# Batch 1 of an FFT-filter and MLP kernel: last first-stage store in two halves, second-stage pieces 0.6 steps later

## The chip, the core and the metric

The kernel runs on one core of one Trainium2 chip. The metric is the device time of one execution in microseconds (us). Before the change the median of three runs is 776.99 us (776.98 to 777.12). The profiler's engines are TensorE (PE, with its weight loads PEld), VectorE (DVE), ScalarE (ACT), GpSimd (POOL) and SyncE (SP). SP only issues DMAs here, and POOL mostly does.

## The reference

Eight sequences of 3008 rows and 256 channels are filtered along the sequence in the frequency domain. The result goes, row by row, through an MLP with a "snake" activation:

```
X = rfft(x, axis=1)                    # x: 8 x 3008 x 256
y = irfft(X * (filt_r + 1j*filt_i))    # 8 x 3008 x 256 -> 24064 rows of 256
h = y @ w_in                           # 256 -> 2048
g = h + sin(alpha*h)**2 / alpha
out = g @ w_out                        # 2048 -> 256, float32
```

## The kernel before

**The filter as matmuls.** A length of 3008 is 47 x 64, so each batch's transform is done in two stages, and its inverse in two more. Batch 0 has a path of its own and stays on chip. Batch 1 goes through HBM twice, by these pieces of the class `Spectral`:

- `first(i)`, i = 0 to 15: one matmul over 47 rows (line 206, tile pa) for two of the 32 row groups, then an eviction by `evac` into the tile t1_h. Four of them make a chunk; the fourth (j == 3) issues the store of the chunk's 8 row groups to the HBM tile d1, on SP (line 211, 384 KB).
- `load_t2(g)`, g = 0 to 3: POOL loads a quarter of d1, turned, into t2 (line 235). As each quarter reads all of d1's row groups, it waits for all four stores.
- `forward(u)`, u = 0 to 11: two matmuls (line 243, tile pb), an ACT eviction into xf (line 246), and two SP copies that swap the halves of xf into xs (line 250).
- `product(u)` and `cross(u)`: three VectorE operations (lines 257, 263, 264) that multiply with the filter and leave p.
- `inverse(u)`: two matmuls of p (line 274, tile pc) and an ACT eviction into g. Every third one issues two SP stores of g to the HBM tile d2 (line 281).
- `load_t4(ch)`: SP loads d2 into t4 (line 306). `last(u)`, u = 0 to 15: the matmuls of the last inverse stage (line 316, tile pd), evicted into y, the MLP's input.

Batches 2 to 7 do the same with packed matmuls in `first_tiled` (line 222, stores at line 229) and `inverse_tiled`. Batch 0's last stage is `last_0` (line 403, tile pd, too). Its late pieces are spread between MLP matmuls one by one.

**The MLP as the beat.** The rows are cut into 48 chunks. `hidden(k, jb)` makes one 128-wide block of the hidden layer: two matmuls (line 601, tile ph), the sine on ACT (line 605, tile cos_all), and VectorE's combination of both into v (line 606). `project(k, u)` makes eight matmuls of the second layer (line 621, tile po). ACT copies finished blocks to o (line 630), and POOL issues their stores to the output (line 665). A *step* is two `hidden` of chunk k and one `project` of chunk k-1 (none in some steps behind a chunk of 384 rows instead of 512, and none in chunk 0). Eight steps make a chunk, so step 18 belongs to chunk 2 and step 38 to chunk 4. In the names of tiles ph_2_4 is block 4 of chunk 2, made in step 18.

**Who sets the order.** All instructions are issued in the order in which the code records them; each engine works through its own in order. Pieces of the batches are put on a list with a due time in steps, by `put`. `slot(at)` runs after a step's hidden pair (at = step) and after its projections (at = step + 0.5), and issues what is due, in order of due time. It stops when a second PE piece turns up that is due later than at - 1, and whatever stands behind that piece waits for the next slot as well. `clear` and `aside` move times a little where a piece of batches 2 to 7 stands close.

For batch 1 the times are: `first(i)` at 6.9 + 0.35 i, `load_t2` at 12.5, `inverse(u)` at inv = 24 + 1.21 u, `forward(u)` at inv - 6, `product(u)` half a step after it and `cross(u)` four steps after it, `load_t4` at 38.5 (three chunks) and 45, `last(u)` from 43 on. Batch 2's first `first_tiled` is due at 37.5.

**Shared buffers.** The pieces' PSUM tiles come in turn from the pool fps, with two buffers; the tiles ph from hps, with four. `first_tiled` takes two of each. A matmul into a buffer waits until the tile before in it has been read: by ACT or VectorE for fps, by VectorE's v for ph.

Of the kernel before, what the change touches and what calls it, by code (L numbers as in the profile page):

```python
# [23 lines left out]
NK = 4 * NS  # L24
# [47 lines left out]
def kernel(  # L72
# [10 lines left out]
    nc = tc.nc  # L83
# [41 lines left out]
    t1_h = [cpool.tile([128, 16, C], FP16, name=f"t1_h{i}") for i in range(2)]  # L125
# [13 lines left out]
    for h in range(2):  # L139
        nc.sync.dma_start(out=x32[:, 4 * C * h:4 * C * h + 4 * C],  # L140
                          in_=bass.AP(tensor=x.tensor, offset=x.offset + 4 * h * C, ap=[[32 * C, 96], [1, 4 * C]]))
# [40 lines left out]
    def evac(dst, src, on_act=None):  # L182
        flip[0] = (flip[0] + 1) % 3
        if flip[0] if on_act is None else on_act:
            marks["act"] = nc.scalar.copy(out=dst, in_=src)  # L185
        else:
            marks["dve"] = nc.vector.tensor_copy(out=dst, in_=src)  # L187

    class Spectral:
# [13 lines left out]
        def first(self, i):  # L203
            ch, j = divmod(i, 4)
            ps = fps.tile([128, 512], FP32, name=f"pa_{self.b}_{i}", tag="f")
            marks["pe"] = nc.tensor.matmul(out=ps[0:NK, :], lhsT=wf_t, rhs=self.x[ch][:, 2 * j:2 * j + 2, :],  # L206
                                           start=True, stop=True)
            r0 = 8 * (ch % 2)
            evac(t1_h[ch // 2][0:NK, r0 + 2 * j:r0 + 2 * j + 2, :], ps[0:NK, :])
            if j == 3:  # L210
                nc.sync.dma_start(out=self.d1_rows[:, 8 * ch:8 * ch + 8, :], 
                                  in_=t1_h[ch // 2][0:NK, r0:r0 + 8, :])

        def first_tiled(self, ch):
            r0 = 8 * (ch % 2)
# [141 lines left out]
    for g in range(2):  # L357
        gs = slice(12 * g, 12 * g + 12)
        for k, filt in enumerate((filt_r, filt_i)):
            for q in range(2):  # L360
                if (g, k, q) == (0, 1, 1):
# [3 lines left out]
                    out=f_t[k][64 * k + 32 * q:64 * k + 32 * q + 32, gs, :],  # L365
                    in_=bass.AP(tensor=filt.tensor, offset=filt.offset + off,
                                ap=[[N1 * C, 32], [step, 12], [1, C]]))
# [167 lines left out]
    for jb in range(0, 16, 8):  # L535
        ins = nc.sync.dma_start(out=w_out32[:, jb:jb + 8],
                                in_=moe_w_out[128 * jb:128 * jb + 1024].rearrange("(b p) c -> p b c", p=128))
# [133 lines left out]
    def put(at, fn, *args, pe=False):  # L671
        pending.append((at, len(pending), pe, fn, args))

    def firsts(b):

        return {2: (37.5, 39.5, 41.5, 43.5), 3: (49.5, 54.5, 60.5, 66.5)}.get(
            b, [48 * b - 105.5 + 8 * ch for ch in range(4)])

    def inverses(b):

        return (63.5, 73.5, 81.5) if b == 2 else [48 * b - 46.5 + 16 * w for w in range(3)]
# [3 lines left out]
    def clear(at):  # L685

        return next((s + 1 for s in bursts if s - 0.75 < at <= s + 0.25), at)

    def aside(at):

        return next((s + 0.05 for s in bursts if s - 1.1 < at <= s), at)
# [9 lines left out]
    for b in range(1, B):  # L701
        s = s1 if b == 1 else Spectral(b)
        z = 48 * b
        if b > 1:
            for ch in range(4):
                put(22 + 4 * ch if b == 2 else firsts(b)[ch] - 8, s.load_x, ch)
        if b < TILED:
            for i in range(16):
                put(6.9 + 0.35 * i, s.first, i, pe=True)
        else:  # L710
            for ch in range(4):
                put(firsts(b)[ch], s.first_tiled, ch, pe=True)
        for g in range(4):
            put(12.5 if b == 1 else 45 if b == 2 else max(70, z - 77 + 12 * g), s.load_t2, g)
        for u in range(12):
            inv = 24 + 1.21 * u if b == 1 else 57 + 2.2 * u if b == 2 else z - 59 + 4 * u
            fwd = inv - 6
            fwd = clear(fwd)
            put(fwd, s.forward, u, pe=True)
            put(aside(fwd + (0.5 if b == 1 else 1.5)), s.product, u)  # L720
            if s.fused:
                put(aside(fwd + (4 if b == 1 else 4.5)), s.cross, u)
            if b < TILED:
                put(inv, s.inverse, u, pe=True)
        if b >= TILED:
            for w in range(3):
                put(inverses(b)[w], s.inverse_tiled, w, pe=True)
        for ch in range(4):
            put(z - (9.5 if b == 1 and ch < 3 else (10.5, 10.5, 10.5, 3)[ch]), s.load_t4, ch)
        for u in range(16):  # L730
            put(clear(z + (u - (5 if b == 1 else 6.5) if u < 4 else 2 * u - 9 if b == 1 else 2.6 * u - 11)),
                s.last, u, pe=True)
# [59 lines left out]
```

## Time and profile before

| what | value |
|---|---|
| median of 3 runs | 776.99 us |
| profiled execution, its own time | 779.76 us |
| its span, first to last instruction | 778.0 us |
| granted TensorE clock, mean | 0.997 |
| HBM traffic over the span | 132 GB/s |
| MLP matmuls, lines 621 and 601, busy | 389.9 us and 389.1 us |
| v on VectorE, line 606, mean of one | 671 ns |
| sine on ACT, line 605, mean of one | 600 ns |
| t2 loads, line 235, median from issue to landing | 5.2 us |

In the lines below, a row of a timeline gives the start in us from the span's start, the duration of the group in us, the engine, the line, the operation with output <- input, the shapes, the count, and in brackets idle time of the engine before it with what ended that. "SPq" is a DMA issue on SP. A row of the waits gives the engine and piece that waited, what it waited for, the total in us, the count and the longest. A row of the windows gives, for a stretch, each engine's busy time in the order PE, PEld, DVE, ACT, POOL, and then the granted clock, the share of the DMA engines' time, and GB/s. Starts of matmuls that follow each other closely overlap by about 0.1 us in the records, so lengths of blocks are read from start to start.

### The profile page before, as it was taken

Reading aid. Unit: us, or ns where it says so; the run is one execution under the profiler, and the core shown is the slowest. Engines: PE = TensorE matmul, PEld = TensorE weight load, DVE = VectorE, ACT = ScalarE, POOL = GpSimd, SP = SyncE. Lnnn points to the kernel's source line nnn. Section 1 sums busy time; section 2 is a strip of 40 time slices with the busy share of each in tenths; the row PEclk is TensorE's granted clock in tenths of the full one; section 3 lists DMA queues with packets and bytes.
Section 4 is the critical chain, followed back from the end, with each engine's and each line's share of the span. In section 5 each row is a group of like instructions: output and inputs, shape, how many; then the busy total and the mean of one; then the engine's idle time right before and its main releaser. Section 6 shows DMA issues by size and latency. Waiting matters only on the chain.

```text
span 778.0 us, 17230 instructions
## 1 busy us (share of the span) xinstructions
PE 764.5 (98%) x6039; PEld 517.0 (66%) x6039; DVE 658.0 (85%) x1174; ACT 610.4 (78%) x1204; POOL 370.4 (48%) x649
## 2 busy tenths in 40 slices
PE   7999999999999999999999999999999999999997
PEld 3757766666666666666666666766666666766665
DVE  6986998999988888898889988898888888787773
ACT  5798888898878877888878787788778787777762
POOL 6355555634555655455464647554454645430000
PEclk9999999999999999999999999999999999999999
DMA  9955578864765428644474536864254322511112
GB/s 223 267 108 160 119 181 242 220 137 124 187 165 133 124 58 219 154 108 127 107 194 121 139 95 145 198 152 120 72 145 110 87 70 56 135 46 34 37 41 56
DMA packets 81518, 101.49 MB, mean 130 GB/s; under 512 B 18884, under 2 KB 60864, under 8 KB 81431
## 3 DMA queue, kind: packets, MB, share of 16 engines
q0 software_dynamic: 27440, 47.29, 26.1%
q1 hardware_dynamic: 53434, 52.79, 25.4%
q8 instruction: 47, 0.77, 0.4%
q10 hardware_dynamic: 557, 0.31, 0.2%
q14 instruction: 40, 0.33, 0.1%
HBM read 56.15 MB, written 46.66 MB: 132 GB/s over the span
## 4 chain that ended last, share of the span: by engine, by line
PE 91%; DVE 5%; ACT 1%; issue 1%; DMA 1%; ACTq 0%; DVEq 0%
PE po L621 40%; PE ph L601 40%; DVE v L606 3%; PE pd L316 2%; PE pb L243 2%; PE pa L222 2%; PE pc L293 1%; ACT cos_all L605 1%; PE pc L513 1%; DMA w<-in_moe_alpha_dram 1%; PE warm L437 1%; PE pb L491 1%; PE pa L459 1%; PE pa L206 0%; PE pd L403 0%
## 5 line engine op out<-in xcount | busy, mean ns | idle before, releaser
L606 DVE SCALAR_TENSOR_TENSOR v<-cos_all,ph 128x512 f16<-128x512 f32 (+1 forms) x768 | 482.5, 671 | 99.2 <-ACT cos_all L605 95.7
L605 ACT ACTIVATE cos_all<-ph 128x512 f32<-128x512 f32 (+1 forms) x768 | 413.9, 600 | 101.8 <-PE ph L601 98.5
L665 POOL DMA_DIRECT2D out_dram<-o x530 | 291.7, 557 | 244.1 <-ACT o L630 215.3
L621 PE MATMUL po<-w,v 128*128 128x256 f16 x3008 | 389.9, 273 | 0.9 <-DVE v L606 0.9
L601 PE MATMUL ph<-y,w 128*128 128x512 f16 (+1 forms) x1536 | 389.1, 375 | 1.3 <-DVE v L606 1.1
L621 PEld LDWEIGHTS <-v 128*128 128x128 f16 x3008 | 289.9, 98 | 85.9 <-DVE v L606 1.5
L601 PEld LDWEIGHTS <-w 128*128 128x128 f16 x1536 | 143.1, 98 | 114.0 <-issue 19.1
L630 ACT COPY o<-po 128x512 f32<-128x512 f32 (+1 forms) x95 | 56.1, 591 | 7.6 <-PE po L621 6.9
L246 ACT CAST xf<-pb 128x512 f16<-128x512 f32 x84 | 51.1, 608 | 2.0 <-PE pb L243 1.2
L185 ACT CAST y<-pd 128x376 f16<-128x376 f32 (+1 forms) x86 | 42.1, 491 | 12.3 <-PE pd L316 8.8
L160 POOL DMA_DIRECT2D x<-in_x_dram x48 | 25.6, 538 | 40.1 <-DVE v L606 26.8
L185 ACT CAST t_h<-pa 128x512 f16<-128x512 f32 (+1 forms) x60 | 32.8, 590 | 12.5 <-PE pa L222 11.3
L316 PEld LDWEIGHTS <-t_a 96*128 96x128 f16 x448 | 31.4, 97 | 12.7
L264 DVE TENSOR_TENSOR p<-p,xs 128x512 f16<-128x512 f16 x84 | 35.7, 425 | 2.9
L263 DVE TENSOR_TENSOR xs<-xs,filt_t 128x512 f16<-128x512 f16 x84 | 35.1, 418 | 1.6 <-DMA xs<-xf 1.6
L257 DVE TENSOR_TENSOR p<-xf,filt_t 128x512 f16<-128x512 f16 x84 | 35.0, 417 | 0.0
L185 ACT CAST gt<-pc 128x512 f16<-128x512 f32 x54 | 28.1, 595 | 8.4 <-PE pc L293 8.4
L187 DVE CAST t_h<-pa 128x512 f16<-128x512 f32 (+1 forms) x52 | 33.5, 682 | 0.2
L243 PE MATMUL pb<-t,d_t 128*128 128x256 f16 x168 | 32.1, 273 | 0.6 <-ACT cos_all L605 0.6
L316 PE MATMUL pd<-wh_t,t_a 96*128 96x94 f16 x384 | 31.8, 204 | 0.0
L235 POOL DMA_DIRECT2D t<-d x28 | 24.4, 874 | 12.0 <-DMA d<-t_h 10.9
L243 PEld LDWEIGHTS <-d_t 128*128 128x128 f16 x168 | 16.3, 98 | 15.1 <-DMA t<-d 0.8
(70 smaller groups left out, 278.0 us busy)
## 6 DMA issues: line engine op xcount, KB each, us to landing
t<-d POOLq DMA_DIRECT2D x28, 384.0 KB, 5.2
xs<-xf SPq DMA_DIRECT2D x168, 64.0 KB
t_a<-d SPq DMA_DIRECT2D x28, 384.0 KB
x<-in_x_dram POOLq DMA_DIRECT2D x50, 188.0 KB, 4.5
d<-t_h SPq DMA_DIRECT2D x48, 192.0 KB
d<-gt SPq DMA_DIRECT2D x36, 256.0 KB
out_dram<-o POOLq DMA_DIRECT2D x91, 64.0 KB, 2.1
out_dram<-o POOLq DMA_DIRECT2D x31, 80.0 KB, 3.6
```

What stands on the lines that cost most here:

```text
L185: marks["act"] = nc.scalar.copy(out=dst, in_=src)
L243: nc.tensor.matmul(out=ps[:, i, :], lhsT=d_t[:, s, :], rhs=self.t2[s // 6][:, s % 6, :], start=True, stop=True)
L246: nc.scalar.copy(out=self.xf[u], in_=ps)
L263: nc.vector.tensor_tensor(out=xs, in0=xs, in1=f_t[1][:, 2 * u:2 * u + 2, :], op=ALU.mult)
L264: nc.vector.tensor_tensor(out=p, in0=p, in1=xs, op=ALU.add)
L316: nc.tensor.matmul(out=psv[:, i, :], rhs=wi_t if self.b < TILED else wh_t, start=True, stop=True, lhsT=t4_h[ch // 2][0:NK, n0 % 16 + i, cb ...
L601: nc.tensor.matmul(out=ps[:, 0:n], lhsT=w1[:, cb, jb * 128:jb * 128 + 128], rhs=y_cols[:, cb, c0:c0 + n], start=(cb == 0), stop=(cb == 1))
L605: nc.scalar.activation(out=cs[:, 0:n], in_=ps[:, 0:n], func=AFT.Sin, bias=float(np.pi / 2))
L606: marks["snake"] = nc.vector.scalar_tensor_tensor(out=v[k][:, jb, 0:n], in0=cs[:, 0:n], scalar=-1.0, in1=ps[:, 0:n], op0=ALU.add, op1=ALU. ...
L621: nc.tensor.matmul(out=pso[k][:, t % 2, :], lhsT=v[k][:, jb, 128 * t:128 * t + 128], rhs=w2[:, jb, :], start=(jb == 0), stop=(jb == 15))
L630: copy(out=o[:, i0:t % 2 + 1, :], in_=pso[k][:, i0:t % 2 + 1, :])
L665: queues[i % len(queues)].dma_start(out=bass.AP(tensor=out.tensor, offset=out.offset + t0 * C, ap=[*ap, [1, C]]), in_=o_blk[p0:p0 + rows, :])
```

## The change

The store of batch 1's last chunk (ch == 3) is issued in two halves of four row groups, the first after the second matmul of the chunk and the second after the fourth. The due time of `inverse(u)` of batch 1 becomes 24.6 + 1.21 u. `forward`, `product` and `cross` are counted from it and so move by 0.6 steps too. Nothing else is edited; the numbers of the lines below `first` rise by two.

```diff
@@ first @@
-            if j == 3:
-                nc.sync.dma_start(out=self.d1_rows[:, 8 * ch:8 * ch + 8, :], 
-                                  in_=t1_h[ch // 2][0:NK, r0:r0 + 8, :])
+            n = 4 if ch == 3 else 8
+            if 2 * j + 2 in (n, 8):
+                n0 = 2 * j + 2 - n
+                nc.sync.dma_start(out=self.d1_rows[:, 8 * ch + n0:8 * ch + n0 + n, :],
+                                  in_=t1_h[ch // 2][0:NK, r0 + n0:r0 + n0 + n, :])
@@ the due times @@
         for u in range(12):
-            inv = 24 + 1.21 * u if b == 1 else 57 + 2.2 * u if b == 2 else z - 59 + 4 * u
+            inv = 24.6 + 1.21 * u if b == 1 else 57 + 2.2 * u if b == 2 else z - 59 + 4 * u
             fwd = inv - 6
             fwd = clear(fwd)
             put(fwd, s.forward, u, pe=True)
             put(aside(fwd + (0.5 if b == 1 else 1.5)), s.product, u)
             if s.fused:
                 put(aside(fwd + (4 if b == 1 else 4.5)), s.cross, u)
             if b < TILED:
                 put(inv, s.inverse, u, pe=True)
```

In the order of instructions that results, the store takes one DMA more on SP. `forward(0)` moves from the first slot of step 18 to the first of step 19, past eight po and four ph matmuls. `forward(1)` moves from the second slot of step 19 to the first of step 20, behind the first matmuls of the second half of `last_0(27)`. The other pieces move by one slot or none. `inverse(11)` moves from slot 37.5 to slot 38, and `first_tiled(0)` of batch 2 from slot 38 to slot 37.5, ahead of the hidden pair of step 38. On SP the two d1 stores of that `first_tiled` now stand ahead of the last two d2 stores of batch 1, and the t4 loads behind both as before.

## The prediction

> **What bounds the kernel now.** I read the page's busy times and chain first.
>
> ```profile
> PE 764.5 (98%) x6039; PEld 517.0 (66%) x6039; DVE 658.0 (85%) x1174; ACT 610.4 (78%) x1204; POOL 370.4 (48%) x649
> PE 91%; DVE 5%; ACT 1%; issue 1%; DMA 1%; ACTq 0%; DVEq 0%
> ```
>
> TensorE (PE) is busy 98% of the span and carries 91% of the chain that ended last. So a change can gain only what it takes out of PE's idle time, and it loses what it puts in. The list of PE's waits between 66 and 200 us, which holds all of batch 1's second stage, is short:
>
> ```profile
> PE pb L243 <- ACT cos_all L605: 0.6, 1, 0.6
> PE pd L403 <- ACT xf L246: 0.4, 1, 0.4
> PE ph L601 <- DVE v L606: 0.2, 1, 0.2
> ```
>
> The timeline around 73 us shows what the first two are:
>
> ```profile
> 69.61 3.34 POOL L235 DMA_DIRECT2D t<-d  x4 [7.16 <-DMA d<-t_h]
> 72.63 0.20 PE L403 MATMUL pd<-wi_t,t_a 128*128 128x94 f16 x1
> 73.44 0.11 PEld L243 LDWEIGHTS <-d_t 128*128 128x128 f16 x2 [0.84 <-DMA t<-d]
> 73.44 0.39 PE L243 MATMUL pb<-t,d_t 128*128 128x256 f16 x2 [0.60 <-ACT cos_all L605]
> 77.73 0.20 PE L403 MATMUL pd<-wi_t,t_a 128*128 128x94 f16 x1 [0.43 <-ACT xf L246]
> ```
>
> POOL issues batch 1's t2 loads (t<-d) at 69.61, when the fourth store of d1 has landed. The trace's landing records give that store issue 64.67, landing 67.64 on fifteen of the DMA engines and 69.02 on the sixteenth; the t2 loads land at 73.39, 75.82, 77.10 and 78.40. The page names ACT's cos for the 0.60 us, but pb needs from ACT only the eviction before it, long done; the weight load on the line above names the load that lands at 73.39. So wait A (0.60 us) is forward(0) waiting for t2. Wait B (0.43 us) is the second half of last_0(27) waiting for a buffer of the two-deep pool fps that forward(1) took just before it and that ACT had not yet emptied.
>
> After that PE is never idle until 135 us, but VectorE has almost nothing left either. The window from step 23 to step 37, then the end of that stretch:
>
> ```profile
> 83.16:111.62 28.46, 28.46 (x209) 20.17 (x207) 28.05 (x60) 25.73 (x51) 14.34 (x28) 1.00 0.73 155
> ```
>
> ```profile
> 110.95 0.42 DVE L263 TENSOR_TENSOR xs<-xs,filt_t 128x512 f16<-128x512 f16 x1
> 111.75 2.47 DVE L606 SCALAR_TENSOR_TENSOR v<-cos_all,ph 128x512 f16<-128x512 f32 x4
> 113.35 0.38 PE L274 MATMUL pc<-p,e_t 128*128 128x256 f16 x2
> 113.57 1.03 PE L601 MATMUL ph<-y,w 128*128 128x512 f16 x4
> 114.53 0.63 PE L222 MATMUL pa<-x,wt_t 47*64 47x512 f16 x8
> 115.97 1.03 PE L601 MATMUL ph<-y,w 128*128 128x512 f16 x4
> ```
>
> In the window row the columns are PE, PEld, DVE, ACT and POOL: PE 28.46 of 28.46 us, DVE 28.05. In the other fence the last inverse of batch 1 (pc, 113.35) comes ahead of the hidden matmuls of step 38 (ph, 113.57) and of batch 2's first first_tiled (pa, 114.53).
>
> **The change, part by part.** (1) *The store in halves.* It adds one DMA on SP, of about 0.32 us issue by the rows of the four stores at L211. SP has nothing else to issue between 64.98 and 74.48, so it costs nothing there; without that cover it would delay the xs copies by 0.3 us, with four steps (8 us) before cross needs them. The first half may go at about 62.1 (the eviction that ends there), the second at 64.7 as now. Nearest rows for its landing: the 384 KB stores issued at 52.84 and 56.80 took 3.00 us each, a 192 KB one at 117.45 took 2.97. So the half lands near 67.7 and the t2 loads issue, with the 0.6 us that POOL took after 69.02, near 68.3 and first land near 72.1 (3.8 us later, as now). Bounds: 72.1 and today's 73.39.
>
> (2) *Second stage 0.6 later.* forward(0) goes from the first half of step 18 to the first half of step 19, past 8 po and 4 ph matmuls. The rows of po and ph give 0.87 us between starts of such blocks, so PE comes to it at 72.83 + 0.87 + 0.87 = 74.6. Both bounds of the landing are earlier: wait A goes by the shift alone, the halves only add room. Gain 0.60.
>
> (3) *The buffer.* forward(1) moves behind the first matmuls of last_0(27)'s second half. That half now takes the buffer of forward(0), evicted a step before, and forward(1) comes some 1.5 us after the po block whose eviction stands ahead of its own buffer's on ACT (two evictions of about 0.5 us each). Wait B goes: 0.43. Bounds 0 and 0.43; I take 0.43. PE is then 1.03 us ahead.
>
> (4) *What VectorE does with that.* DVE's work in the stretch is the same, but begins with the shifted pieces. By DVE's rows (v pairs at 95.29, 97.61, 99.94) a step with a v pair and cross, cross, product takes 2.33 us, so 1.20 for the pair and 1.13 for the three; a step with cross alone 1.99 (105.78, 107.77), so 0.79. In the new order the stretch runs from v of step 23 to v of step 37: 15 pairs, 9 triples, 3 crosses = 18.0 + 10.2 + 2.4 = 30.5 us. PE reaches step 23 at 83.16 - 1.03 = 82.13; v can follow 1.40 us behind ph (89.24 to 90.64, with one ACT eviction ahead), 83.5. So DVE ends v of step 37 at 114.1. Now it ends at 111.75 + 2.47 = 114.22: DVE keeps its place while PE has moved forward.
>
> The new order has one consequence more: inverse(11) falls from slot 37.5 to 38, and first_tiled(0) of batch 2 goes ahead of step 38's hidden pair. It takes two of the four hps buffers, so that pair needs those of step 37's pair, free when DVE has finished its v at 114.1. PE alone would start the second of the pair at: ph of step 37 110.6 (111.62 - 1.03), less the 0.22 of inverse(10) that now follows it, 110.4; + 0.87 + 0.22 + 0.87 + 0.63 + 0.43 = 113.4. It waits until 114.2, some 0.75 us. After it come 0.43 + 0.22 + 0.87, so step 39 starts at 115.7 against 115.97 now. I take 0.25 us ahead, that is 0.78 lost of the 1.03. Bounds: nothing lost (if v starts earlier or its row of triples is broken) and all of it.
>
> On the way, cross(4) ends about 0.1 us ahead of inverse(4), the tightest of the twelve; its cost is 0 to 0.2, and I take 0, for DVE then sets the end of the stretch anyway.
>
> (5) *The t4 loads.* SP's order turns too:
>
> ```profile
> 117.45 1.90 SPq L229 DMA_DIRECT2D d<-t_h  x2
> 119.58 1.74 SPq L306 DMA_DIRECT2D t_a<-d  x3
> 126.28 0.35 PEld L316 LDWEIGHTS <-t_a 96*128 96x128 f16 x4
> ```
>
> Now d2's last stores are issued at 114.38 and 115.02, land at 117.94, and the t4 loads go out at 119.58, the first landing at 124.80; last(1) uses it at 126.28. After: the two casts of pa follow v (114.1 + 1.28 = 115.4), the two d1 stores issue by 116.7 to 117.4, d2's stores behind them by 118.0 to 118.7, landing at 121.0 to 121.7 (2.92 us after issue at 115.02; queued behind the d1 stores' data). The three t4 loads wait for this, and d1 stores of chunk 1 queue behind them on SP; nobody needs those before t2 of batch 2, whose first use is ten microseconds later. A first t4 load of a later batch lands 3.74 to 4.65 us after issue, today's 5.22: 124.7 to 126.9. PE will want it at 126.28 - 0.25 = 126.0. I take 125.6, no wait; bounds 0 and 0.9.
>
> [...]
>
> **The sum.** -0.60 - 0.43 + 0.78 + 0 + 0 = -0.25 us, on the profiled execution's span of 778.0 (its time 779.76, so 1.8 lies around it). The runs shown have a median of 776.99, 2.8 below the profiled one; a microsecond of PE's is worth the same in both. PE has only 0.2 + 0.4 us idle from 135 to 700, so the lead passes to the end. 776.99 - 0.25 = 776.7.
>
> **The rivals.** *The lead stays whole:* DVE's chain does not bind at step 38. For it: step 23's v may come 1.26 us behind ph (81.20 to 82.46), and PE finds no wait there today. Against: 28.05 busy of 28.46. Then 776.99 - 1.03 = 776.0.
>
> *The t4 load is late:* last(1) waits on the store-then-load chain of SP. It decides once the first t4 load lands after 126.0; each microsecond behind that is a microsecond of PE. At today's 5.22 us latency it lands at 126.9: 776.74 + 0.9 = 777.6, slower than before. If one DMA engine is also late, as the sixteenth was at 69.02 (1.38 us), 779.0. For it: the two transfers now run one after the other, where today's t4 loads merely queued. Against: the common 4.3 us latency just makes it.
>
> *Nothing comes of it:* another wait takes the places of A and B near 75 us (forward(1) behind a late ACT eviction, or the xs copies colliding with the t2 loads on the DMA engines), and DVE's wait then is smaller. 776.99 again.
>
> **How the numbers follow.** Forecast 0.50, lead whole 0.22, t4 late 0.20, nothing 0.08. The range 775.9 to 777.9 takes in the first two, the fourth, and the third without its late engine; about 0.15 is left out. Within 0.2% (1.55 us, about what a measurement of this kernel can tell from no change) lie all four but for the late engine: same 0.89. Faster by 1.55 would need more idle PE time than A and B hold: 0.05. Slower by 1.55 is the tail of the t4 case: 0.06.
>
> **What would show it.** Right: no PE wait at pb L243's first start (about 74.6) nor at last_0(27); a PE wait for DVE's v of some 0.7 us near 113 to 114, ahead of the hidden pair that follows pa; t4 loads issued near 121.5; PE's first pd of batch 1 within 0.5 us of 126.2. Wrong: pb still waiting for t<-d; no wait for v near 114; a wait of over 0.3 us at pd L316, or a new wait in a later batch.

## The result, and the profile after

| | before | after |
|---|---|---|
| median | 778.08 us (776.96 to 779.04, 14 runs) | 780.10 us (778.28 to 784.06, 14 runs) |
| profiled execution: span | 778.0 us | 782.2 us |
| profiled execution: granted TensorE clock | 0.997 | 0.994 |

The ratio of after to before is 1.0036, 95% interval 1.0020 to 1.0052. The change costs about 2 us by the medians (2.8 us by the ratio), where 0.25 us of gain was forecast. The time is also above the range's upper end, 777.9. Of the 3.4 us between the 776.7 forecast and this, 1.1 is not the change's: before, measured again beside it, has a median of 778.08, where the forecast started from 776.99. One of e2's eight executions below, 790.16 us at a mean granted clock of 0.991, counts as slow and is left out of e2's figures.

The page's busy times and chain of after, the same two lines as shown of before:

```profile
PE 767.8 (98%) x6039; PEld 518.3 (66%) x6039; DVE 658.3 (84%) x1174; ACT 611.8 (78%) x1204; POOL 370.6 (47%) x649
PE 82%; DVE 8%; DMA 5%; ACT 2%; issue 1%; POOL 1%; SPq 0%; DVEq 0%; POOLq 0%; ACTq 0%
```

PE runs the same 6039 matmuls but is busy 3.3 us longer (767.8 against 764.5): some of them ran slower (four ph matmuls at 147.20 took 1.89 us, four of before at 143.25 took 1.03). The chain that ended last now goes through DMA for 5% of the span, against 1%. Listed in order of time (start, length in us), it has these pieces between 125 and 147 us; of before's chain, no DMA is listed there. They are two of the transfers that the rest of this text is about:

```profile
125.36 8.10 DMA d<-t_h
134.10 1.33 POOL t L237 x2
137.96 8.20 DMA x<-in_x_dram
```

The list of PE's waits from 66 to 200 us has this:

```profile
PE pa L224 <- DMA x<-in_x_dram: 2.7, 2, 2.4
PE ph L603 <- DVE v L608: 0.4, 2, 0.2
```

Waits A and B of before (pb L243, 0.6; pd L403, 0.4) are both gone. A new one stands in their place: `first_tiled` waits 2.7 us for an x load. PE's timeline shows where: first the row of before, without a wait, then those of after. The windows of after (PE, PEld, DVE, ACT and POOL busy, then the granted clock) show what came behind the wait:

```profile
145.07 0.63 PE L222 MATMUL pa<-x,wt_t 47*64 47x512 f16 x8
```

```profile
145.38 0.56 PE L224 MATMUL pa<-x,wt_t 47*64 47x512 f16 x2 [2.38 <-DMA x<-in_x_dram]
146.20 1.06 PE L224 MATMUL pa<-x,wt_t 47*64 47x512 f16 x6 [0.27 <-DMA x<-in_x_dram]
```

```profile
138.00:145.40 7.40, 5.02 (x38) 3.12 (x36) 4.47 (x8) 4.89 (x10) 3.65 (x7) 1.00 1.03 287
145.50:152.30 6.80, 6.53 (x29) 3.01 (x28) 3.76 (x7) 3.69 (x7) 5.12 (x10) 0.50 0.89 217
152.40:160.00 7.60, 7.60 (x60) 5.24 (x59) 6.14 (x12) 5.65 (x11) 2.49 (x5) 1.00 0.30 72
```

This is step 55, the x-transform of batch 3's chunk 1. PE stands for 2.38 and 0.27 us. Right behind the first gap the granted clock is 0.50 for 6.83 us (145.50 to 152.32 by the trace's clock records), in which PE ran 29 matmuls in 6.80 us, against 60 in the 7.60 us after it; half of 6.83, 3.41 us, is taken as lost. Together 2.65 + 3.41 = 6.06 us.

Both traces have a hidden pair at each step, so they can be laid on each other at step 16 (67.67 us before, 65.86 after; the difference arises at start-up, where before's execution has a half-clock piece of its own, 0.50 from 8.70 to 12.11 us). From there PE of after is ahead by 1.15 us at step 24, 0.49 at step 39 and 0.34 at step 54. It is 5.72 behind at step 58 (0.34 - 6.06 = -5.72), and that is not won back. Another 0.78 is lost in steps 158 to 160, near 350 us, and leaves it 6.49 behind at step 380. That second loss does not come from the late x: e1, e4, e7 and e9 lose 0.62 to 0.78 there as well, some of them without a late x, and in all five VectorE waits 1.6 to 1.8 us for an xs copy there.

Why x is late stands in the queues of POOL and SP. POOL of before, then of after:

```profile
133.09 3.34 POOL L235 DMA_DIRECT2D t<-d  x4 [3.77 <-DMA d<-t_h]
136.42 1.11 POOL L160 DMA_DIRECT2D x<-in_x_dram  x2
```

```profile
134.10 3.34 POOL L237 DMA_DIRECT2D t<-d  x4 [7.08 <-DMA d<-t_h]
137.43 1.10 POOL L160 DMA_DIRECT2D x<-in_x_dram  x2
```

POOL stops at batch 2's t2 loads (t<-d) until the d1 stores of batch 2 have landed, 7.08 us now. The two x loads of batch 3's chunk 1 stand behind them and need nothing of d1. And SP: of before, the two rows on either side of those that the prediction shows, then after:

```profile
114.38 1.26 SPq L281 DMA_DIRECT2D d<-g  x2
121.43 6.83 SPq L229 DMA_DIRECT2D d<-t_h  x6
```

```profile
113.37 1.28 SPq L231 DMA_DIRECT2D d<-t_h  x2
114.75 1.45 SPq L283 DMA_DIRECT2D d<-g  x2
119.58 1.28 SPq L308 DMA_DIRECT2D t_a<-d  x3
120.95 6.40 SPq L231 DMA_DIRECT2D d<-t_h  x6
```

As the prediction has it, batch 1's last d2 stores (d<-g) now stand behind the first d1 stores. The three t4 loads wait for them until 119.58, and the six d1 stores of batch 2's chunks 1 to 3 follow. Those are held up in turn, not on SP but after their issue: the last is issued at 125.36 and lands at 133.45, 8.10 us later.

### The profile page after: what moved, and what is told of

Its sections match the earlier page's. It is cut to its first block, busy times and chain, and to the rows that moved or that the text cites. A ratio compares the mean times of both kernels' runs of the same rounds, so it can differ in the third digit from the quotient of the medians.

```text
span 782.2 us, 17234 instructions
## 1 busy us (share of the span) xinstructions
PE 767.8 (98%) x6039; PEld 518.3 (66%) x6039; DVE 658.3 (84%) x1174; ACT 611.8 (78%) x1204; POOL 370.6 (47%) x649
## 4 chain that ended last, share of the span: by engine, by line
PE 82%; DVE 8%; DMA 5%; ACT 2%; issue 1%; POOL 1%; SPq 0%; DVEq 0%; POOLq 0%; ACTq 0%
PE po L623 37%; PE ph L603 36%; DVE v L608 6%; PE pd L318 2%; PE pb L245 2%; PE pa L224 1%; DMA w<-id 1%; PE pc L295 1%; DMA x<-in_x_dram 1%; DMA d<-t_h 1%; DMA xs<-xf 1%; ACT cos_all L607 1%; DVE xs L265 1%; DVE p L266 1%; DVE p L259 1%
```

## The experiments

The theory: the 0.6 steps turn the order of `inverse(11)` and `first_tiled(0)` in step 38; this puts the t4 loads later; d1 of batch 2, its t2 loads, and the x loads behind these on POOL each come late in turn; PE waits at step 55, and the clock falls behind the wait. The rivals: the store in halves loads the DMA engines; or the lead itself is at fault, PE coming to x too early.

This table is worked out from each profiled execution: issues and landings by the trace's DMA records, PE by its first pa of that chunk. All are us from the first hidden matmul of step 16 of the same execution.

| kernel | last d2 store issued | first t4 load issued | last d1 landed | x issued | x landed (two halves) | PE starts |
|---|---|---|---|---|---|---|
| before | 47.35 | 51.91 | 64.87 | 68.75 | 75.09, 76.27 | 77.41 |
| after | 49.55 | 53.72 | 67.60 | 71.57 | 79.48, 80.30 | 79.52, waits 2.7 |
| e1, halves alone | 46.55 | 50.98 | 64.83 | 68.80 | 75.20, 76.49 | 76.63 |
| e2, 0.6 steps alone | 49.59 | 53.77 | 67.66 | 71.55 | 80.37, 81.32 | 80.42, waits 3.6 |
| e3, old order kept | 46.75 | 51.72 | 65.40 | 69.38 | 75.81, 77.21 | 76.83 |
| e4, new order alone | 51.13 | 54.99 | 67.66 | 71.56 | 78.45, 79.68 | 78.49, waits 0.8 |
| e8, 0.18 steps | 46.56 | 51.58 | 65.12 | 69.10 | 75.69, 77.10 | 76.63 |
| e10, 0.18 steps, x ahead | 46.56 | 51.02 | 65.78 | 61.87 | 69.13, 70.19 | 76.63 |

And the times, each with the kernel before on the same chip. The last column counts executions whose mean granted clock was below 0.999. Before has some too: 3 of the 31, 6 of the 35 and 5 of the 23 beside the experiments.

| kernel | median, us (runs) | before, us (runs) | ratio, 95% interval | clock below 0.999 |
|---|---|---|---|---|
| after | 780.10 (14) | 778.08 (14) | 1.0036, 1.0020 to 1.0052 | 6 of 14 |
| e1 | 777.15 (12) | 777.71 (31) | 0.9997, 0.9980 to 1.0014 | 1 of 12 |
| e2 | 781.50 (7) | 777.71 (31) | 1.0044, 1.0028 to 1.0059 | 4 of 7 |
| e3 | 777.84 (12) | 777.71 (31) | 1.0001, 0.9989 to 1.0013 | 3 of 12 |
| e4 | 781.67 (12) | 778.02 (35) | 1.0031, 1.0005 to 1.0057 | 6 of 12 |
| e5 | 777.36 (13) | 777.71 (31) | 0.9990, 0.9977 to 1.0004 | 1 of 13 |
| e6 | 780.47 (12) | 778.02 (35) | 1.0024, 1.0007 to 1.0040 | 5 of 12 |
| e7 | 782.16 (12) | 778.02 (35) | 1.0048, 1.0032 to 1.0065 | 9 of 12 |
| e8 | 777.28 (12) | 778.02 (35) | 0.9980, 0.9966 to 0.9994 | 1 of 12 |
| e9 | 777.68 (12) | 778.58 (23) | 0.9996, 0.9974 to 1.0019 | 2 of 12 |
| e10 | 776.74 (12) | 778.58 (23) | 0.9978, 0.9965 to 0.9991 | 0 of 12 |

### One part of the change at a time (e1, e2)

e1 is the changed kernel with the old times; e2 is the kernel before with the new times:

```diff
-            inv = 24.6 + 1.21 * u if b == 1 else ...
+            inv = 24 + 1.21 * u if b == 1 else ...
```

```diff
-            inv = 24 + 1.21 * u if b == 1 else ...
+            inv = 24.6 + 1.21 * u if b == 1 else ...
```

> The store in halves alone, due times as before. Order theory (the loss comes from inverse(11) falling behind first_tiled(0) of batch 2, which puts batch 2's later d1 stores on SP behind the t4 loads' wait, so that the t2 loads of batch 2 and the x load of batch 3's chunk 1 behind them on POOL come late): that order is as before, so no PE wait for x near 145 us and a full granted clock there. The t2 loads of batch 1 issue about 1.5 us earlier and PE's 0.6 us wait at forward(0) shrinks or goes: 0 to 0.6 us faster than before. Lead theory (the x load is late because PE runs ahead of the transfers): a lead of 0.6 us takes half of the 1.1 us by which the x load lands ahead of its use before the change; no wait yet. Store theory (the halves themselves do harm): about 2 us slower than before.

> The due times 0.6 later alone, the store in one piece. Order theory: the same swap in step 38, so PE waits 1 to 3 us for x near 145 us, with a drop of the granted clock behind it in part of the runs, and the time is within 1 us of the changed kernel, about 2 us slower than before. Lead theory: the same. Store theory: no loss, 0 to 1 us faster than before.

The halves alone cost nothing measurable. In e1's execution wait A is gone and only wait B is left of the two; PE keeps a lead of 0.78 us over before from step 20 to step 55, and x is in time. That the halves made this lead is not shown: e7 below is the kernel before up to this stage, and its execution has no wait A and the same lead. There batch 1's last d1 store took 3.08 us to land, where before's took 4.35. The 0.6 steps alone make the whole loss (1.0044), with the wait for x as in after. So it is not the halves.

### The order of step 38 (e3, e4)

e3 keeps the 0.6 steps, but holds `inverse(11)` ahead of slot 37.5, so that the order of step 38 is the old one. e4 does the opposite: the kernel before with the new order of step 38 and nothing else.

```diff
-                put(inv, s.inverse, u, pe=True)
+                put(min(inv, 37.4), s.inverse, u, pe=True)
```

```diff
-                put(inv, s.inverse, u, pe=True)
+                put(37.91 if u == 11 else inv, s.inverse, u, pe=True)
```

> The changed kernel with inverse(11) due at 37.4 at the latest, which puts it and its d2 stores ahead of batch 2's first first_tiled again. Order theory: the t4 loads issue some 2 us earlier against PE, the d1 stores behind them too, the t2 loads of batch 2 and the x load likewise; no wait for x of over 0.3 us, no clock drop, and the lead of forward(0) and last_0(27) is kept: 0.3 to 1.1 us faster than before, 2 to 3 us faster than the changed kernel. Lead theory: PE is still some 1 us ahead, so x still comes late by 0 to 1 us and the time stays 0 to 3 us above before.

> The kernel before, with nothing but the order of step 38 changed: inverse(11) of batch 1 is put behind first_tiled(0) of batch 2 (due 37.91 in place of 37.31), as the shift of 0.6 steps does. No store in halves, no lead of TensorE from the earlier steps. Order theory: the last d1 store of batch 2's chunk 1 is issued behind the t4 loads and lands 2 to 3 us later than before, batch 2's t2 loads (their 7 us wait on POOL) and the x load of batch 3's chunk 1 behind them come 1 to 3 us later, TensorE waits 0.5 to 3 us for that x near step 55 (145 us), and the time is 1 to 4 us above before (ratio 1.001 to 1.005). Theory that the lead itself is what upsets the later stage (TensorE reaching the load's first use earlier): no wait for x, time as before (0.999 to 1.001).

With the old order the loss is gone (1.0001) though the shift is still there; with the new order alone it is there (1.0031) though no lead exists. As the cause of the loss, the lead falls on both. In e4's execution the wait for x is 0.8 us, less than in after: PE itself is 1.05 us later than before at step 39, and x lands 0.6 to 1.0 us earlier than in after. Of its 3.9 us of span over before's, the new order makes 1.6 by step 58 (0.5 in step 38, 1.1 at x); 0.5 is a longer wait A (1.1 us for t2), 0.8 the place near 350 us, and 1.0 its start and end. The clock does not fall at x in this execution (1.00 from 135 to 160 us); its low mean comes from start-up (0.94 over the first 30 us). Five more of e4's executions have a low clock, and their cause is not shown.

SP's rows of e4 are those of after in another place:

```profile
117.04 1.28 SPq L229 DMA_DIRECT2D d<-t_h  x2
118.44 1.43 SPq L281 DMA_DIRECT2D d<-g  x2
122.96 1.26 SPq L306 DMA_DIRECT2D t_a<-d  x3
124.32 5.51 SPq L229 DMA_DIRECT2D d<-t_h  x6
```

The table gives the link in between. In before, after, e1 to e4 and e8, where the order from the first t4 load to the last d1 store is the same, the last d1 store lands 12.7 to 13.9 us after the first t4 load is issued. Its own issue hardly moves (59.98 before, 59.50 after, 59.21 in e1): what is late is its data. Of after's 2.7 us against before, 1.8 is the later issue of the t4 loads, and 0.9 a longer stretch from there (13.88 us against 12.96). So a d2 store issued 2.2 us later puts d1's landing 2.7, x's issue 2.8 and x's landing 4.0 to 4.4 us later (after against before; the first x load itself took 7.9 us, against 6.3).

### Undoing one late transfer each (e5, e6)

Both are the changed kernel. e5 puts the x loads of batch 3's chunk 1 ahead of the t2 loads on POOL; e6 gives the three t4 loads of batch 1 a later due time, to bring them behind the d1 stores of chunk 1 on SP.

```diff
-                put(22 + 4 * ch if b == 2 else firsts(b)[ch] - 8, s.load_x, ch)
+                put(22 + 4 * ch if b == 2 else 44.9 if (b, ch) == (3, 1) else firsts(b)[ch] - 8, s.load_x, ch)
```

```diff
-            put(z - (9.5 if b == 1 and ch < 3 else (10.5, 10.5, 10.5, 3)[ch]), s.load_t4, ch)
+            put(z - (8.4 if b == 1 and ch < 3 else (10.5, 10.5, 10.5, 3)[ch]), s.load_t4, ch)
```

> The changed kernel with one x load (batch 3, chunk 1) due at 44.9, so that POOL issues it ahead of batch 2's t2 loads. Order theory and lead theory alike: that x load lands 10 us before its use, PE's wait for it goes, and with it the drop of the granted clock; what is left is the lead at step 39, 0.3 to 0.8 us faster than before. The t2 loads come 1 us later; batch 2's forward(0) may wait up to 0.5 us. If the clock drops on its own: the granted clock is still halved near 145 us in part of the runs and the time stays about 2 us above before.

> The changed kernel, with the three early t4 loads of batch 1 due 1.1 steps later (39.6 in place of 38.5), so that the d1 stores of batch 2's chunk 1 go ahead of them on SP again. Order theory: d1 lands near 131 us, the x load of batch 3's chunk 1 is issued by 136.5 and landed by 144.2 us, TensorE does not wait for it, and the time is 776.5 to 778 (ratio to before 0.998 to 1.001); the t4 loads land some 2 us later than now, which their first use at 124 us just allows or turns into a wait of up to 1.5 us. If the swap of the two pairs on TensorE, and not the queue behind it, is the cause: the wait for x of 2 us and the loss of 3 us stay (1.003 to 1.005).

In neither does PE wait for x, but a late transfer is found elsewhere. A row of PE's timeline of e5, then one of e6:

```profile
142.78 0.39 PE L245 MATMUL pb<-t,d_t 128*128 128x256 f16 x2 [3.43 <-DMA t<-d]
```

```profile
126.15 0.34 PE L318 MATMUL pd<-wi_t,t_a 96*128 96x94 f16 x4 [2.09 <-DMA t_a<-d]
```

e5 shows that x's place behind the t2 loads is what makes it late: with x ahead, the median is 777.36. But its profiled execution is the slowest of its 13 (783.65 us). There d1 lands at 69.17, and now batch 2's `forward(0)` waits for t2 itself. e6 misses its expectation on the time. By its trace the two d1 stores of chunk 1 come ahead of the t4 loads as meant, the four of chunks 2 and 3 behind them ("again" was wrong: before has all six behind). x is issued at 70.00, 1.6 us earlier than in after, and is in time. But `last(1)` waits 2.09 us for a t4 load, the wait that the prediction priced as a rival for the change itself; with the half clock behind it (a mean of 0.72 from 126 to 132 us), PE loses 3.84 us between steps 39 and 54. The ratio is still 1.0024. In the new order of step 38, the traces of e5 and e6 each show the delay moved to another of these transfers: x, t2 or t4.

### The late x by itself (e7)

The kernel before, with x of that chunk due at 48.1, on POOL behind other issues:

```diff
-                put(22 + 4 * ch if b == 2 else firsts(b)[ch] - 8, s.load_x, ch)
+                put(22 + 4 * ch if b == 2 else 48.1 if (b, ch) == (3, 1) else firsts(b)[ch] - 8, s.load_x, ch)
```

> The kernel before, with one load moved: x of batch 3's chunk 1 is due at step 48.1 in place of its own place 8 steps ahead of its use, so POOL issues it later, behind other issues; nothing else changes, no swap and no lead. Theory that the late x with what follows it (the wait, and the clock halved behind the wait in part of the executions) makes the whole loss: TensorE waits 2 to 5 us at the x-transform of that chunk, the granted clock falls to half for 3 to 7 us behind it in part of the executions, and the time is 2 to 8 us above before (ratio 1.003 to 1.010). Theory that the wait is absorbed later and the loss lies elsewhere: the wait shows in the trace, but the time is within 1 us of before (0.999 to 1.001).

```profile
145.88 0.64 PE L222 MATMUL pa<-x,wt_t 47*64 47x512 f16 x2 [3.38 <-DMA x<-in_x_dram]
147.28 1.06 PE L222 MATMUL pa<-x,wt_t 47*64 47x512 f16 x6 [0.76 <-DMA x<-in_x_dram]
```

PE's timeline of e7 has the wait of after, somewhat longer, and the clock is halved for the same 6.83 us (145.49 to 152.32). The ratio is 1.0048. A late x, with the old order and the old due times, is enough for a loss of this size. This execution does have a lead over before's, 0.78 us, because wait A did not come up in it; e1, e8 and e10 have the same lead and no such loss.

### A shift that keeps the order (e8, e9, e10)

`inverse(11)` stays ahead of slot 37.5 as long as the shift is below 0.19. e8 is the changed kernel with 0.18, e9 the kernel before with 0.18 (the store whole), e10 is e8 with e5's line for x.

```diff
-            inv = 24.6 + 1.21 * u if b == 1 else ...
+            inv = 24.18 + 1.21 * u if b == 1 else ...
```

> The changed kernel with the shift cut to 0.18 steps (24.18 in place of 24.6): inverse(11) stays due ahead of step 37.5, so the order of step 38 and of the SP queue is that of before, while the store in halves stays. Order theory: no wait for x near step 55, the wait for t2 at forward(0) is gone (as with the halves alone), the wait at last_0(27) gone or 0.4 us as before; time 776.3 to 777.8 (ratio 0.998 to 1.000). Theory that any shift of the pieces costs: 1.001 to 1.005.

> The kernel before with the shift of 0.18 steps alone (24.18 in place of 24), the store whole. Step 38 keeps its order. If the small shift makes what the halves with it made: the wait for t2 at forward(0) is gone or under 0.3 us, no wait for x near step 55, and the ratio to before is 0.997 to 1.000, as with the halves (0.998). If the halves are needed for it: forward(0) still waits 0.3 to 0.6 us for t2 and the ratio is 0.999 to 1.001. Order theory in either case: no loss, because the order of step 38 is that of before.

> The halves with the shift of 0.18 steps, and the x load of batch 3's chunk 1 due at 44.9, ahead of batch 2's t2 loads on POOL. If the stage from 110 to 146 us still loses time to an x that is now and then late, this takes it away: time 776 to 777.3, no execution above 780 for a low clock. If x was always in time at 0.18 steps: as without it, 776.8 to 777.8. If the load ahead delays the t2 loads instead: batch 2's forward(0) waits 1 to 3.5 us for t2 in part of the executions, and the time is 777.5 to 781.

e8 and e10 are faster than before with intervals that leave out 1: 0.9980 and 0.9978. In e10 all twelve executions lie between 776.44 and 777.66 us, where before ran from 776.62 to 782.49 beside it. PE's waits of e10 from 66 to 200 us are two:

```profile
PE pd L405 <- ACT xf L248: 0.4, 1, 0.4
PE ph L603 <- DVE v L608: 0.2, 1, 0.2
```

Wait A is gone, B has stayed, x has 6 us of room (landed at 70.19, used from 76.63). In e8 the second half of x lands at 77.10, 0.47 us after PE has started on the first, and PE's second part of that chunk starts at 77.14: it waits for it (in e10 both parts start together), and the lead falls from 0.78 to 0.43. The same happens in e3 and e9 (0.58 to 0.31, 0.78 to 0.39). So a lead of 0.6 to 0.8 us does use up x's room, and this much of the theory of the lead is right: it costs 0.3 to 0.4 us, not 6. e9 has no wait A either, but as e7 lost it without any shift, this does not show that the 0.18 steps took it away. e9's interval (0.9974 to 1.0019) doesn't tell it from before, nor from e8. What the halves are worth in e8 stays open.

## Why the prediction was wrong

The mechanisms of its steps 1 to 4 and most numbers of step 5 hold. The predicted times below are in before's count, so 1.81 us (67.67 - 65.86) is added to those of after.

1. *The halves cost nothing:* shown by e1 (0.9997).
2. and 3. *Waits A and B go, 1.03 us:* both are gone in after, and the lead at step 24 is 1.15. `forward(0)`'s pb starts at 72.60 + 1.81 = 74.41 (74.6 forecast). That the shift alone is enough and the halves "only add room" is borne out by e2: there, without the halves, the first t2 load lands as late as in before (5.91 us behind the start of step 16, against 5.73), and `forward(0)` starts at 6.74 without a wait. What was not seen is that wait A is no fixed property of before: it was read from one execution, and in e7's, the same up to there, it is absent (t2 landed at 4.56, pb started at 5.00). So the 0.60 is gained only in part of the executions.
4. *VectorE and the new order of step 38 take back 0.78, 0.25 is left:* 0.49 is left at step 39, so 0.66 of the 1.15 was taken back. The mechanism is the one forecast: VectorE ends v of step 37 at 112.09 (113.90 in before's count, 114.1 forecast), and the second ph of the pair starts right behind it. The one listed wait is 0.25 us, not 0.75; the rest is in matmuls that follow each other more slowly. From the start of pa to that of ph it takes 1.07 us, where before's pa (114.53) was followed after 0.56:

```profile
110.48 0.82 PE L224 MATMUL pa<-x,wt_t 47*64 47x512 f16 x8
111.55 1.19 PE L603 MATMUL ph<-y,w 128*128 128x512 f16 x4 [0.25 <-DVE v L608]
```

5. *The t4 loads:* the last d2 store is issued at 117.21 and lands at 121.34 (118.0 to 118.7 and 121.0 to 121.7 forecast); the t4 loads go out at 121.39; the first lands at 124.93 (125.6 taken); PE starts pd at 125.95 without a wait (126.0). The landing of d2 came out right by luck: the issue was at least 0.8 us earlier than forecast, and the transfer took 4.13 us in place of 2.92. The rest is as forecast.

The step that failed is the sentence in step 5: "The three t4 loads wait for this, and d1 stores of chunk 1 queue behind them on SP; nobody needs those before t2 of batch 2, whose first use is ten microseconds later." Its last clause looks at who uses the data, and not at who stands behind the one that waits for it. POOL's t2 loads wait for d1, and x of batch 3's chunk 1 stands behind them on POOL. The trace of before showed it all: the wait of POOL at 133.09 for d1, the x issues right behind it at 136.42, and x landing at 142.76 and 143.94 for a use at 145.07, 1.1 us of room. In after x landed 4.0 to 4.4 us later. The prediction counted this wait only for t4, where it found 0.4 us of room. That "the lead passes to the end" was true of PE's idle time as it stood, and fell with this. Among its signs of being wrong the prediction did name "a new wait in a later batch", without a price or a chance. Where the order stays it is partly borne out: e1, e8 and e10 all have a lead of 0.78 us at step 54; at step 200 e10 still has 0.78, e8 0.43 (the second half of its x was a little late), e1 0.03 (its VectorE waits 1.8 us for an xs copy near 342 us).

The second thing that it left out is the price. It took each microsecond of a late load for a microsecond of PE. Here 2.65 us of waiting cost 6.06 in the profiled execution, because the clock was halved behind it. By the clocks of the other executions this does not happen each time: of after's 14 executions, the six with a mean clock below 0.999 have a median of 782.6 us, the other eight 779.7.

## What to carry to other kernels

When a step is moved, follow its DMAs past the data's first user: here POOL's t2 loads waited 7.08 us for d1, and the x loads behind them, which need nothing of d1, were issued 2.8 us later than before. Write down for each transfer behind such a wait when it lands and when it is used; here the room was 1.1 us in a trace in which PE showed no wait at that place. A load that needs nothing of what POOL waits for can be issued ahead of that wait (e5, and e10, where x landed 6.4 us ahead of its use), though that is not free: d1 then landed 1.6 us later in e5's trace than in after's, and 0.7 later in e10's than in e8's. And check whether a shift turns the order of two pieces: 0.18 steps kept it here, 0.6 did not.

## What was not expected of the hardware

The granted clock fell to 0.50 behind gaps of PE of 2.09 us (e6), 2.38 (after), 3.08 (e2), 3.38 (e7) and 3.43 (e5), and stayed there for 3.41 us (e2, e5, e6) or 6.83 (after, e7). Two executions lost it at start-up too, for 3.41 us: before, behind a gap of 1.70, and e4, behind gaps of 0.68 and 1.23. Yet e8's gap of 1.29 had no such effect, nor had e4's of 1.11 and 0.83 later on. So the length of a single gap does not decide.

The stretches between changes of the clock are whole multiples of 3.41 us in the clock records of before and after, at full clock too: after's 139.95 us from 5.55 to 145.50 are 41 of them and its 628.05 us from 152.32 on 184, before's 764.59 us from 12.11 on 224. If each of the twelve traces is cut into such pieces from its first clock record on, and PE's idle time is added up in each piece, the pieces right ahead of these seven falls hold 1.78 us (before), 1.85 (e2), 1.91 (e4), 2.09 (e6), 2.25 (e5), 2.38 (after) and 2.98 us (e7); those ahead of the twelve falls at the program's end hold 2.1 to 3.4. Of all other pieces, one holds 1.78 us (e2, the piece ahead of the one with 1.85) and none more than 1.5. In these runs, then, the idle time within a piece went with the half clock, but no sharp line shows: a piece with 1.78 us was followed by it in before, and not in e2. e2's gap of 3.08 us lies in two pieces, 1.78 us in the one and 1.30 in the next; with a second gap of 0.55 in the latter, the clock fell behind it. Why only a part of the executions lose the clock is not shown by any run here.
